# A spectral filter kept and loaded in two halves: forward and backward of a GFNet mixer and a token MLP on one core

## The chip, the core and the metric

The kernel runs on one core of a Trainium2 chip. A core has five engines that run side by side, each with its own instruction queue: TensorE (PE in the profile, its weight loads PEld), VectorE (DVE), ScalarE (ACT), GpSimd (POOL) and SyncE (SP), which here only issues DMAs. ScalarE and GpSimd can issue DMAs too. The DMAs of all of them are carried out by the core's 16 DMA engines. The metric is the device time of one execution in microseconds (us), as the median of several runs.

## The reference, cut to what matters

Forward and backward of two residual blocks over x of 2048 x 448 (bf16). The first block multiplies the two-dimensional real Fourier transform of the normalised input by a complex filter `w_r + 1j * w_i` of 2048 x 225; the second is an MLP over the 2048 tokens.

```python
def _A_ref(x, w_r, w_i):
    X = rfft2(x.astype(float32), axes=(-2, -1))
    W = w_r + 1j * w_i
    X = X * W
    return irfft2(X, s=(S, D), axes=(-2, -1)).astype(bfloat16)

x = A_x
h = x + _A_ref(_layernorm(x), A_w_r, A_w_i)
h2 = h + _B_ref(_layernorm(h), B_w1, B_b1, B_w2, B_b2)   # LN, w1, gelu, w2
_out, _vjp = jax.vjp(_f, A_x, A_w_r, A_w_i, B_w1, B_b1, B_w2, B_b2)
return (out, *vjp(grad_out))
```

The outputs are the result and the gradients of x, w_r, w_i (out_2 and out_3), w1, b1, w2 and b2.

## The kernel before

The transforms are written as matrix products. The forward transform has two parts. In the **row steps** (a loop over t = 0 to 15, lines 932 to 979) PE turns sixteen row tiles of the normalised input with `row_a` and `row_b`; the factor rstd of each tile is scaled into a 128 x 128 matrix by `scale_R` on VectorE, and for tiles 6 to 15 it comes from `newton_gp`, ten small GpSimd instructions for each pair of tiles (lines 410 to 416 in the profile). `fold_prep` and `fold_quarters` on VectorE prepare the operand of two tiles. Every second `row_b` ends with a **row move**, a DMA from SBUF to SBUF into `D2` (line 697), issued by SyncE and, for the last one, by ScalarE. Then comes the **spectral stage** `s2_stage` (line 704): in sets s = 0 to 3 of four groups each, PE transforms down the columns (`four`, 32 x 32 products, line 225), the callback `fwd_mult` multiplies by the filter on VectorE (`w_mult`, two products of 128 x 900 and two sums of 128 x 450, twice a set), PE transforms back, and the results are moved into `D3` by DMAs that GpSimd issues (line 740; in the last set SyncE and ScalarE issue three of the four). Set s uses the groups 8*(s//2) + s%2 + 2a, a = 0 to 3: sets 0 and 1 use groups 0 to 7, sets 2 and 3 groups 8 to 15. After it the inverse row transforms, the MLP, and the same transforms backward follow; there `bwd_mult` also writes the filter's gradient in place over the filter, and it is stored in the last stage.

Between the stages PE is kept going with `fill(n)`, which issues n matmuls of another product, here `dg_gen` (the product of w2 and grad_out, 224 matmuls). Its operand w2 comes in fourteen blocks, five loaded plainly and turned by PE, nine loaded by DMA transposes that SyncE issues (line 312), in a ring of five slots; `cap` holds the later ones back until the row steps are done, and `held_w2` is then emptied.

The instructions of PE, VectorE, ScalarE and SyncE run in the order in which the program writes them. GpSimd's order is chosen by the framework's planner, which simulates the program.

The **filter** lies in `rW`, as component, group and column for each of 128 partitions. `w_io` is a generator that makes one DMA at each `next`; it serves the loads (line 597, from `W_AT` in the row steps) and, at the end, the stores of the gradient (from `GW_AT` in `gx_consumer`). The 64 even partitions hold 16 consecutive rows each, one piece of 7200 bytes; the odd ones hold the mirrored rows, 450 bytes a piece. The move of 16 rows for group 0 of the first odd partitions is the tail. Of the 18 loads 14 are issued by SyncE, and four by GpSimd, each held by a VectorE memset of one element that it overwrites (line 596).

```python
for _ in range(W_AT.get(t, 0)):
    next(w_loads, None)
```

Of the kernel before, what the change touches and what calls it, by code (L numbers as in the profile page):

```python
# [17 lines left out]
P = 128  # L18
S = 2048
D = 448  # L20
DF = 225
# [4 lines left out]
NG = 16  # L26
# [77 lines left out]
class Ring:  # L104
# [7 lines left out]
    def next(self):  # L112
        v = self.views[self.i % len(self.views)]
        self.i += 1
        Ring.release(v)
        return v
# [8 lines left out]
def kernel(  # L125
# [20 lines left out]
    nc = tc.nc  # L146
# [4 lines left out]
    gp_ = nc.gpsimd  # L151
# [9 lines left out]
    def region(name, n):  # L161
        return mem.tile([P, n], BF16, name=name)

    def cut(reg, off, *dims):
        n = int(np.prod(dims))
        v = reg[:, off:off + n]
        if len(dims) == 1:
            return v
        names = "abcd"[:len(dims)]
        return v.rearrange("p (" + " ".join(names) + ") -> p " + " ".join(names),  # L170
                           **{c: d for c, d in zip(names, dims)})
# [59 lines left out]
    def set_of(v, s):  # L231
        return v.rearrange("p (e a c) x k -> p e c a x k", e=2, a=4, c=2)[:, s // 2, s % 2]
# [16 lines left out]
    rW = region("rW", NG * 2 * KW)  # L249
# [157 lines left out]
    def newton_gp(v, y, sl):  # L407
        vi, yi = nt_i[:, 0, sl], y.bitcast(I32)
        a = nt_f[:, 0, sl]
        gp_.tensor_scalar(out=v, in0=v, scalar1=LN_EPS, scalar2=None, op0=ALU.add)  # L410
        gp_.tensor_scalar(out=yi, in0=v.bitcast(I32), scalar1=-0.5, scalar2=RSQRT_MAGIC, op0=ALU.mult, op1=ALU.add)
        for c0, c1 in RSQRT_STEPS:
            gp_.tensor_tensor(out=a, in0=y, in1=y, op=ALU.mult)
            gp_.tensor_tensor(out=a, in0=a, in1=v, op=ALU.mult)
            gp_.tensor_scalar(out=a, in0=a, scalar1=c0, scalar2=c1, op0=ALU.mult, op1=ALU.add)
            gp_.tensor_tensor(out=y, in0=a, in1=y, op=ALU.mult)
# [141 lines left out]
    def gen_inv_d(ch):  # L558
        e, en = inv_cols[ch]
        pt = ps_ff()[:].bitcast(BF16)[:, 0:2 * 2 * P].rearrange("p (w b c) -> p w b c", w=2, b=2)  # L560
        for w in range(2):
            for b in range(2):
                nc.tensor.transpose(pt[0:KC, w, b, :], csF[:, w, b, DC * ch:DC * ch + KC], ident[:])
        for w, x in ((0, e), (1, en)):
            for b in range(2):
                lo = D - DC - DC * b
                for o, i_, f in ((DC * b, pt[0:KC, w, b, 0:DC], e), (lo, pt[0:KC, w, b, DC - 1::-1], x)):
                    o = csI[0:KC, w, ch, o:o + DC]
                    if w:
                        ve.tensor_scalar(out=o, in0=i_, scalar1=f[0:KC], scalar2=None, op0=ALU.mult)  # L570
                    else:
                        sc.activation(out=o, in_=i_, func=ACT.Copy, scale=f[0:KC])

    Wc = cut(rW, 0, 2, NG, DF)
    W = Wc.rearrange("p c g k -> p g c k")

    def w_io(dr, di, store):
        Wq = Wc.rearrange("(q s) c g k -> s q c g k", s=2)  # L580
        for c_, d in ((0, dr), (1, di)):
            moves = []
            for i in range(4):
                moves.append((Wq[0][16 * i:16 * i + 16, c_].rearrange("l g k -> l (g k)"), 16 * i, [[P * DF, 16], [1, 16 * DF]]))
                g0 = 0 if i else 1
                moves.append((Wq[1][16 * i:16 * i + 16, c_, g0:NG, :], P - 16 * i - g0,
                              [[P * DF, 16], [-DF, NG - g0], [1, DF]]))
            moves.append((Wq[1][0:16, c_, 0, :], 64, [[P * DF, 16], [1, DF]]))
            late = [m for n, m in enumerate(moves) if n in (0, 2, 4, 6)] if c_ and not store else []
            early = moves if not late else [m for n, m in enumerate(moves) if n not in (0, 2, 4, 6)]  # L590
            for n, (sb, row, dims) in enumerate(early + late):
                d_ap = bass.AP(d.tensor, d.offset + row * DF, dims)
                eng = nc.sync if n < len(early) else gp_
                if eng is gp_:
                    i = 32 * (n - len(early))
                    nc.vector.memset(Wc[i:i + 1, 1, 8, 0:1], 0.0)
                eng.dma_start(out=d_ap if store else sb, in_=sb if store else d_ap)
                yield

    r452_ring = ring(r452, 0, 8, 2, KW)  # L600
    Xs = cut(rX, 0, NG, 2, KW)
# [151 lines left out]
    def w_mult(xc, w, y, conj):  # L753
        wr = w[:, :, 0:1, :].broadcast_to([P, 2, 2, DF])
        wi = w[:, :, 1:2, :].broadcast_to([P, 2, 2, DF])
        p1, p2 = (p_ring.next()[:, :, :, 0:DF] for _ in range(2))
        xc, y = xc[:, :, :, 0:DF], y[:, :, :, 0:DF]
        ve.tensor_tensor(out=p1, in0=xc, in1=wr, op=ALU.mult)
        ve.tensor_tensor(out=p2, in0=xc, in1=wi, op=ALU.mult)
        ve.tensor_tensor(out=y[:, :, 1, :], in0=p1[:, :, 0, :], in1=p2[:, :, 1, :],  # L760
                         op=(ALU.add if conj else ALU.subtract))
        ve.tensor_tensor(out=y[:, :, 0, :], in0=p1[:, :, 1, :], in1=p2[:, :, 0, :],
                         op=(ALU.subtract if conj else ALU.add))
# [37 lines left out]
    def fill(n):  # L801
        while n > 0 and pending:
            try:
                next(pending[0])
                n -= 1
                if row_ops:
                    row_ops.pop(0)()
            except StopIteration:
                pending.pop(0)
# [12 lines left out]
    def load_biases():  # L822
        gp_.memset(smr, 0.0)
        nc.sync.dma_start(out=gtail[:, 0:64], in_=grad_out[0][S - 16:S, 3 * P:D])
        nc.sync.dma_start(out=smr[0:NFB, 0, :], in_=B_b1.rearrange("(j p) -> j p", p=P))
        nc.sync.dma_start(out=smr[:, 1, :], in_=B_b2.rearrange("(j p) -> j p", p=P))

        def turn():
            for i, dst in ((0, b1col), (1, b2col)):
                nc.sync.dma_start_transpose(out=smc[:, i, :], in_=smr[:, i, :])  # L830

        def place():
            for i, dst in ((0, b1col), (1, b2col)):
                ve.tensor_copy(out=dst[:], in_=smc[:, i, :])
        return turn, place
# [65 lines left out]
    w_loads = w_io(A_w_r, A_w_i, False)  # L901
# [19 lines left out]
    GROUPS = {0: (6, 8), 1: (8, 10), 3: (10, 12), 5: (12, 14), 7: (14, 16)}  # L921
    STATS = {0: (6, 7), 1: (8, 9), **{t: (t + 8,) for t in range(2, 8)}}
    INV_S = {11: 0, 12: 1, 13: 2, 14: 3}
    W_AT = {**{t: 2 for t in range(6)}, 6: 6}
    FILL_A = (4, 4, 8, 12, 6, 3, 3, 4, 5, 3, 3, 2, 2, 2, 3, 3)
    FILL_B = (0, 0, 2, 2, 2, 2, 4, 4, 3, 2, 2, 2, 2, 2, 2, 2)
    def uv_step():
# [4 lines left out]
    for t in range(NT):  # L932
# [34 lines left out]
        if t in GROUPS:  # L967
            a, b = GROUPS[t]
            newton_gp(mvx[:, a:b, 1], rstd_x[:, a:b], slice(a, b))
        for _ in range(W_AT.get(t, 0)):  # L970
            next(w_loads, None)
        if t in INV_S:
            gen_inv_s(INV_S[t])
        if t == 13:
            for c in range(2):
                for e in range(2):
                    sc.copy(out=Rp.rearrange("p (e a q b c) -> p c e a q b", e=2, c=2, q=8, a=2)[:, c, e],
                            in_=Rm[:, 64 * c + 32 * e:64 * c + 32 * e + 32].rearrange("p (q a b) -> p a q b", q=8, a=2))
        fill(FILL_B[t])
    for _ in uv:  # L980
        pass
    for _ in w_loads:
        pass
    gp_.memset(csF[:, 0, :, 0:1], 1.0)
    gen_inv_d(0)
    fill(6)
    gen_inv_d(1)
    turn_biases, place_biases = load_biases()
    cap[0] = NFB
    while held_w2:  # L990
        held_w2.pop(0)()
    fill(4)
    gen_RT()
    fill(7)

    def fwd_mult(s, j, x, y):
        w_mult(x, set_of(W, s)[:, 2 * j:2 * j + 2], y, False)

    s2_stage(lambda s: set_of(Xs, s), fwd_mult, 8, (8,) * 5, 0, split=True)
    sc.activation(out=warm, in_=eps_h, func=ACT.Sqrt)  # L1000
# [99 lines left out]
    for jp in range(NFB // 2):  # L1100
# [27 lines left out]
        d = Later(ve, om_ops) if jp >= NFB // 2 - 2 else ve  # L1128
# [141 lines left out]
    def load_xall(q):  # L1270
        nc.sync.dma_start(out=xall[:, 4 * q:4 * q + 4, :], in_=x_pt[:, 4 * q:4 * q + 4, :])
# [8 lines left out]
    for t in range(NT):  # L1280
# [6 lines left out]
        pb, tmp, m1, m2, _ = ln_a(t, pdh[:, 0:D], rstd_h[:, t:t + 1], hln[:, t, :], (1.0 + LN_EPS) / D)  # L1287
# [10 lines left out]

    def bwd_mult(s, j, xc, y):
        xs = set_of(Xs, s)[:, 2 * j:2 * j + 2, :, 0:DF]  # L1300
        gw = set_of(W, s)[:, 2 * j:2 * j + 2]
        w_mult(xc, gw, y, True)
        xc = xc[:, :, :, 0:DF]
        p1, p2 = (p_ring.next()[:, :, :, 0:DF] for _ in range(2))
        ve.tensor_tensor(out=p1, in0=xc, in1=xs[:, :, 0:1, :].broadcast_to([P, 2, 2, DF]), op=ALU.mult)
        ve.tensor_tensor(out=p2, in0=xc, in1=xs[:, :, 1:2, :].broadcast_to([P, 2, 2, DF]), op=ALU.mult)
        ve.tensor_tensor(out=gw[:, :, 0, :], in0=p1[:, :, 0, :], in1=p2[:, :, 1, :], op=ALU.add)
        ve.tensor_tensor(out=gw[:, :, 1, :], in0=p1[:, :, 1, :], in1=p2[:, :, 0, :], op=ALU.subtract)
# [77 lines left out]
    Meter.slack = 2.0  # L1386
    g_out = w_io(out_2, out_3, True)
    X_AT = {0: 2, 4: 3}
    GW_AT = tuple(range(12)) + tuple(range(1, 12, 2))

    def gx_consumer(t, py):
        if t in X_AT:
            load_xall(X_AT[t])
        for _ in range(GW_AT.count(t)):
            next(g_out, None)
# [87 lines left out]
```

## Time and profile before

| | us |
|---|---|
| median of three runs | 342.39 (342.36 to 346.57) |
| the profiled execution, its own time | 340.34 |
| its span, first to last instruction | 338.3 |

| stretch of the profiled execution | from | to |
|---|---|---|
| filter loads issued by SyncE (14) | 11.5 | 38.5 |
| filter loads issued by GpSimd (4) | 28.6 | 31.1 |
| last row moves issued | 42.2 | 45.4 |
| bias loads issued by SyncE (3) | 45.4 | 47.6 |
| last five w2 transposes issued | 47.7 | 65.0 |
| spectral stage, first to last PE step (line 225) | 48.4 | 69.2 |
| filter gradient stored (18 DMAs) | 289.2 | 321.2 |

A line of the timeline gives the start, the length, the engine and line, the operation, what it writes and reads, how often, and in brackets how long its engine had been idle before it and who ended that. "SPq" and "POOLq" are instructions of a queue that issue or wait. The length of a DMA line is the time that its issue took the queue, not the transfer; the time to landing stands in another view. A line of the stretches gives the bounds and the length, and then for PE, PEld, DVE, ACT and POOL the busy time and the number of instructions, then PE's granted clock, the DMA share and GB/s. Line 84 is a helper through which all of VectorE's and ScalarE's instructions go, line 220 that of the large matmuls, line 225 that of the small ones. Of the tiles, rX holds scaled matrices and later the forward transform, r stands for small regions, rS for work space, rO and rE for w2 blocks.

### The profile page before, as it was taken

The page shows a single profiled execution, that of the slowest core. Times are in us where ns is not written, and L with a number is a line of the kernel's source. Part 1 is how long each engine was busy: PE and PEld are TensorE (multiplying, and loading weights), DVE is VectorE, ACT ScalarE, POOL GpSimd, SP SyncE. Part 2 cuts the span into 40 slices and gives each one's busy share as a digit, 9 for nine tenths or more (in the row PEclk, how much of TensorE's full clock was granted, in tenths as well). Part 3 has the DMA queues.
Part 4 walks back from the last instruction along what each step waited for, and adds up shares of the span by engine and source line. Part 5 has one row for each costly group of instructions (what it writes and reads, how often), then busy time and mean ns, then how long its engine had stood idle before and what let it go on. Part 6 is the DMA issues. An engine that isn't in the chain of part 4 may idle for free.

```text
span 338.3 us, 7987 instructions
## 1 busy us (share of the span) xinstructions
PE 330.2 (98%) x2893; PEld 174.6 (52%) x2893; DVE 251.7 (74%) x670; ACT 206.7 (61%) x448; POOL 84.6 (25%) x254
## 2 busy tenths in 40 slices
PE   8999989999999999999999999999999999999995
PEld 4666554456545555555555555554344434555552
DVE  8998739827947888593227888786697993599994
ACT  6987666848965534423222346665588875588882
POOL 7767202412210000000001111210020222156670
PEclk9999999999999999999999999999999999999999
DMA  7999899959899999687877889837699999978885
GB/s 251 400 203 182 190 258 141 227 125 279 230 378 287 348 279 242 179 274 192 193 178 164 174 188 155 176 84 232 221 220 302 290 244 252 284 188 278 245 293 200
DMA packets 136198, 78.03 MB, mean 231 GB/s; under 512 B 86528, under 2 KB 127592, under 8 KB 136032
## 3 DMA queue, kind: packets, MB, share of 16 engines
q1 hardware_dynamic: 133288, 73.13, 84.5%
q0 software_dynamic: 2448, 3.83, 5.3%
q8 instruction: 22, 0.36, 0.5%
q10 hardware_dynamic: 424, 0.58, 0.5%
q14 instruction: 16, 0.13, 0.1%
HBM read 28.33 MB, written 22.04 MB: 149 GB/s over the span
## 4 chain that ended last, share of the span: by engine, by line
PE 83%; DVE 6%; DMA 4%; ACT 3%; issue 1%; POOL 1%; SPq 0%; DVEq 0%; ACTq 0%
PE ps_mm L220 68%; PE ps_ff L220 9%; PE ps_ff L225 3%; DMA r<-r 3%; ACT rO L84 2%; PE ps_mm L375 2%; DVE rS L84 2%; DVE r L84 1%; DMA r<-rX 1%; DVE rX L84 1%; DVE stats L84 1%; DVE rA L84 1%; ACT rE L84 1%; PE ps_mm L318 0%; DVE rG L84 0%
## 5 line engine op out<-in xcount | busy, mean ns | idle before, releaser
L220 PEld LDWEIGHTS <-r 128*128 128x128 bf16 (+2 forms) x628 | 58.6, 105 | 48.5 <-issue 3.0
L220 PEld LDWEIGHTS <-rS 128*128 128x128 bf16 (+1 forms) x468 | 36.2, 97 | 31.9 <-issue 6.0
L84 ACT CAST rO<-ps_mm 128x512 bf16<-128x512 f32 (+1 forms) x68 | 36.5, 584 | 14.5 <-PE ps_mm L220 11.9
L220 PE MATMUL ps_mm<-rD,r 128*128 128x448 bf16 x224 | 44.5, 352 | 0.0
L220 PEld LDWEIGHTS <-rst 128*128 128x128 bf16 (+1 forms) x320 | 23.9, 97 | 30.4 <-issue 12.1
L740 POOL DMA_DIRECT2D r<-r x29 | 17.4, 605 | 67.3 <-ACT r L84 56.7
L220 PE MATMUL ps_mm<-rC,rE 128*128 128x448 bf16 x144 | 32.1, 353 | 0.0
L220 PE MATMUL ps_mm<-rB,r 128*128 128x448 bf16 x160 | 31.2, 352 | 0.2 <-DVE rB L84 0.2
L220 PE MATMUL ps_mm<-rG,rst 128*128 128x512 bf16 (+1 forms) x128 | 28.5, 380 | 0.0
L220 PE MATMUL ps_mm<-r,rst 128*128 128x512 bf16 (+2 forms) x144 | 27.3, 345 | 0.0
L84 ACT ACTIVATE r<-ps_mm,rstd_h 128x448 bf16<-128x448 f32 x16 | 10.1, 634 | 26.8 <-PE ps_mm L220 26.8
L84 DVE SCALAR_TENSOR_TENSOR r<-ps_mm,b2col,r 128x448 bf16<-128x448 f32 x16 | 10.9, 682 | 19.9 <-PE ps_mm L220 18.6
L84 ACT ACTIVATE r<-rC 128x448 bf16<-128x448 bf16 x16 | 9.1, 570 | 26.7 <-DMA out_dram<-r 13.8
L84 ACT CAST r<-ps_ff 128x452 bf16<-128x452 f32 x43 | 23.1, 592 | 3.1 <-PE ps_ff L220 1.2
L1220 POOL TENSOR_SCALAR lcol<-lcol 128x1 f32<-128x1 f32 x16 | 8.5, 530 | 64.7 <-ACT r L84 64.7
L84 ACT ACTIVATE rG<-rG 128x896 bf16<-128x896 bf16 x14 | 13.3, 950 | 14.9 <-DVE rG L84 14.7
L220 PEld LDWEIGHTS <-rO 128*128 128x128 bf16 (+1 forms) x165 | 15.4, 98 | 12.3 <-ACT rO L84 0.2
L84 ACT CAST rS<-ps_ff 128x512 bf16<-128x512 f32 x31 | 18.0, 583 | 4.2 <-PE ps_ff L220 4.2
L220 PE MATMUL ps_ff<-csI,rAT 113*128 113x224 bf16 (+1 forms) x108 | 19.0, 298 | 0.2 <-DVE rA L84 0.2
L84 ACT CAST rG<-ps_mm 128x512 bf16<-128x512 f32 (+1 forms) x28 | 14.0, 539 | 7.6 <-PE ps_mm L220 7.5
L84 ACT CAST rAT<-ps_ff 113x512 bf16<-113x512 f32 x24 | 13.9, 586 | 7.7 <-PE ps_ff L220 7.5
L84 DVE TENSOR_SCALAR rG<-rG 128x896 bf16<-128x896 bf16 x28 | 10.9, 389 | 10.0 <-ACT rG L84 10.0
(200 smaller groups left out, 647.4 us busy)
## 6 DMA issues: line engine op xcount, KB each, us to landing
out_dram<-rO SPq DMA_DIRECT2D x34, 256.0 KB, 3.3
r<-in_B_w_dram SPq DMA_DIRECT2D x5, 1024.0 KB, 9.1
r<-r POOLq DMA_DIRECT2D x29, 113.0 KB, 5.5
out_dram<-rG SPq DMA_DIRECT2D x11, 256.0 KB, 3.1
r<-in_B_w_dram SPq DMA_DIRECT2D x3, 896.0 KB, 5.6
rS<-in_B_w_dram SPq DMA_DIRECT2D x3, 896.0 KB
rB<-in_B_w_dram SPq DMA_DIRECT2D x5, 512.0 KB, 8.1
r<-r SPq DMA_DIRECT2D x11, 226.0 KB, 2.5
```

The costliest lines, as they stand in the source:

```text
L84: fn(**kw)
L220: nc.tensor.matmul(out, lhsT=lhsT, rhs=rhs, start=start, stop=stop)
L225: nc.tensor.matmul(out, lhsT=lhsT, rhs=rhs, start=start, stop=stop)
L375: nc.tensor.matmul(idle[:, 0:D], lhsT=rAT[:, 0:P], rhs=rAT[:, 0:D], start=True, stop=True)
L740: defer(RESH_LAG, lambda g=g, ab=ab, eng=eng: eng.dma_start(out=D3[rowbase(g):rowbase(g) + 29:4, :, :, :], in_=ab), ab)
L1220: gp_.tensor_scalar(out=m1, in0=ms, scalar1=-1.0 / D, scalar2=None, op0=ALU.mult)
```

## The change

The filter is kept as two halves of eight groups, each with both components: half 0 serves sets 0 and 1, half 1 sets 2 and 3. `w_set(s)` gives the view that `set_of(W, s)` gave. `w_io` goes through half 0 and then half 1; in each it moves, for each component, all 64 even-partition rows in one DMA (pieces of 3600 bytes; the DRAM side has the dimensions 4, 16 and the piece), then four DMAs of the odd partitions, and in half 0 the tail. That is 22 DMAs instead of 18. In the row steps `W_AT` now takes the twelve of half 0, all from SyncE, in steps 0 to 8. The ten of half 1 stand behind the row steps, after the table scaling `gen_inv_d` and after the held w2 loads; two are issued by SyncE and eight by GpSimd, and all are held by one VectorE memset of two elements in each partition. The bias loads move behind them. The stores are taken from `GW_AT` as before, but 22 of them, all from SyncE.

```diff
-    Wc = cut(rW, 0, 2, NG, DF)
-    W = Wc.rearrange("p c g k -> p g c k")
+    Wc = rW[:, 0:2 * NG * DF].rearrange("p (e c g k) -> p e c g k", e=2, c=2, g=NG // 2)
+
+    def w_set(s):
+        return Wc[:, s // 2].rearrange("p c (a b) k -> p b a c k", b=2)[:, s % 2]
 
     def w_io(dr, di, store):
-        Wq = Wc.rearrange("(q s) c g k -> s q c g k", s=2)
-        for c_, d in ((0, dr), (1, di)):
-            moves = []
-            for i in range(4):
-                moves.append((Wq[0][16 * i:16 * i + 16, c_].rearrange("l g k -> l (g k)"), 16 * i, [[P * DF, 16], [1, 16 * DF]]))
-                g0 = 0 if i else 1
-                moves.append((Wq[1][16 * i:16 * i + 16, c_, g0:NG, :], P - 16 * i - g0,
-                              [[P * DF, 16], [-DF, NG - g0], [1, DF]]))
-            moves.append((Wq[1][0:16, c_, 0, :], 64, [[P * DF, 16], [1, DF]]))
-            late = [m for n, m in enumerate(moves) if n in (0, 2, 4, 6)] if c_ and not store else []
-            early = moves if not late else [m for n, m in enumerate(moves) if n not in (0, 2, 4, 6)]
-            for n, (sb, row, dims) in enumerate(early + late):
-                d_ap = bass.AP(d.tensor, d.offset + row * DF, dims)
-                eng = nc.sync if n < len(early) else gp_
-                if eng is gp_:
-                    i = 32 * (n - len(early))
-                    nc.vector.memset(Wc[i:i + 1, 1, 8, 0:1], 0.0)
-                eng.dma_start(out=d_ap if store else sb, in_=sb if store else d_ap)
-                yield
+        Wq = Wc.rearrange("(q s) e c g k -> s q e c g k", s=2)
+        H = NG // 2
+        for e in range(2):
+            for c_, d in ((0, dr), (1, di)):
+                up, dn = Wq[0][:, e, c_], Wq[1][:, e, c_]
+                moves = [(up.rearrange("q g k -> q (g k)"), H * e, [[16 * DF, 4], [P * DF, 16], [1, H * DF]])]
+                for i in range(4):
+                    g0 = 0 if e or i else 1
+                    moves.append((dn[16 * i:16 * i + 16, g0:H], P - 16 * i - H * e - g0,
+                                  [[P * DF, 16], [-DF, H - g0], [1, DF]]))
+                if not e:
+                    moves.append((dn[0:16, 0], 64, [[P * DF, 16], [1, DF]]))
+                for n, (sb, row, dims) in enumerate(moves):
+                    eng = gp_ if e and n and not store else nc.sync
+                    d_ap = bass.AP(d.tensor, d.offset + row * DF, dims)
+                    eng.dma_start(out=d_ap if store else sb, in_=sb if store else d_ap)
+                    yield
...
-    W_AT = {**{t: 2 for t in range(6)}, 6: 6}
+    W_AT = {0: 2, 1: 1, 2: 2, 3: 1, 4: 2, **{t: 1 for t in range(5, 9)}}
...
-    for _ in w_loads:
-        pass
     gp_.memset(csF[:, 0, :, 0:1], 1.0)
     gen_inv_d(0)
     fill(6)
     gen_inv_d(1)
-    turn_biases, place_biases = load_biases()
     cap[0] = NFB
     while held_w2:
         held_w2.pop(0)()
+    nc.vector.memset(Wc[:, 1, :, 0, 0:1], 0.0)
+    for _ in w_loads:
+        pass
+    turn_biases, place_biases = load_biases()
...
-    GW_AT = tuple(range(12)) + tuple(range(1, 12, 2))
+    GW_AT = tuple(range(12)) + tuple(range(1, 11))
```

More of the change, by code (lines that the diff above doesn't have):

```diff
@@ L996, in fwd_mult @@
     def fwd_mult(s, j, x, y):
-        w_mult(x, set_of(W, s)[:, 2 * j:2 * j + 2], y, False)
+        w_mult(x, w_set(s)[:, 2 * j:2 * j + 2], y, False)
     s2_stage(lambda s: set_of(Xs, s), fwd_mult, 8, (8,) * 5, 0, split=True)
@@ L1300, in bwd_mult @@
         xs = set_of(Xs, s)[:, 2 * j:2 * j + 2, :, 0:DF]
-        gw = set_of(W, s)[:, 2 * j:2 * j + 2]
+        gw = w_set(s)[:, 2 * j:2 * j + 2]
         w_mult(xc, gw, y, True)
```

## The prediction

> **What bounds the kernel now.** First the page's engine table, then the chain that ended last, then the timelines of GpSimd, VectorE and SyncE's queue around the filter loads, then stretches of PE.
>
> ```profile
> PE 330.2 (98%) x2893; PEld 174.6 (52%) x2893; DVE 251.7 (74%) x670; ACT 206.7 (61%) x448; POOL 84.6 (25%) x254
> ```
>
> PE is all but full and its order is fixed, so a change that leaves PE's work alone gains only where PE stands or drags. The stretches say where: PE idles 0.68 us in 32-36, 0.06 in 36-40, 0.52 in 44-48 and 0.39 in 48.0-48.4: 1.65 us between the row steps and the first step of the spectral stage.
>
> ```profile
> 32.00:36.00 4.00, 3.32 (x37) 1.89 (x38) 2.57 (x10) 2.99 (x6) 2.65 (x14) 1.00 1.00 203
> 44.00:48.00 4.00, 3.48 (x22) 1.78 (x20) 1.92 (x10) 2.50 (x10) 0.04 (x1) 1.00 0.95 334
> ```
>
> The chain (start, length, what) names the cause: from 34.0 to 36.2 it runs through GpSimd's rstd steps, then a VectorE fold, and at the end through the last row move.
>
> ```profile
> 33.59 0.41 PE ps_ff L220 x4
> ...
> 35.97 0.21 POOL rstd_x L416
> ...
> 36.20 0.89 DVE rX L84 x2
> ...
> 43.01 1.23 DVE rX L84 x2
> 44.24 0.47 SPq L697
> ...
> 44.81 3.45 DMA r<-rX
> ...
> 48.40 0.72 PE ps_ff L225 x24
> ```
>
> GpSimd's timeline has the four filter loads inside that rstd work; VectorE waits behind it twice; SyncE's queue is busy without a break from 37.3 to 65.
>
> ```profile
> 28.57 1.76 POOL L597 DMA_DIRECT2D rW<-in_A_w_i_dram  x3
> 30.54 0.53 POOL L597 DMA_DIRECT2D rW<-in_A_w_i_dram  x1
> 33.38 0.25 DVE L84 TENSOR_SCALAR rX<-Rm,rstd_x 128x128 bf16<-128x128 bf16 x1 [0.81 <-POOL rstd_x L416]
> 36.20 0.32 DVE L84 TENSOR_SCALAR rX<-Rm,rstd_x 128x128 bf16<-128x128 bf16 x1 [0.78 <-POOL rstd_x L416]
> 39.29 2.78 SPq L312 DMA_TRANSPOSE rO<-in_B_w_dram  x1
> 42.17 1.23 SPq L697 DMA_DIRECT2D r<-r  x2
> 59.47 1.17 DVE L84 TENSOR_TENSOR rS<-rX,rW 128x900 bf16<-128x900 bf16 x2
> ```
>
> **Row steps.** Removed: four GpSimd loads (1.76 + 0.53 = 2.3 us) and four one-element VectorE fills (0.41 us at 27.97). The rstd group of tiles 12-13 had begun at 26.66 and lacked three steps at 28.57; without the loads it ends near 29.5 instead of 33.35, so the first VectorE wait (0.81) goes. The PE stall at 35.02 (0.66 us, ended by the fold behind that wait) goes with it: 0.7 us. The group of tiles 14-15 needs statistics that come at 31.3, takes ten steps of some 0.28 us, and could end near 34.2 instead of 36.17. That frees the second wait (0.78), and the fold before PE at 38.44, where weights waited 0.50 us: I take 0.5. Against it: GpSimd's order is the planner's, and a memset of csF that waits for PE (34.05, after 0.56 idle) sits in this group. If it still cuts in before the last seven steps, the 0.5 is 0. So 1.2 us, bounds 0 and 2.1 (PE's 1.65 idle plus 0.5 hidden in pipelined records).
>
> **SyncE's queue in the row steps.** 14 loads become 12, nine ahead of the third w2 transpose instead of twelve (3 x 0.62 = 1.9 us of issue less), and one, the last, falls between the fourth transpose (39.29) and the five back-to-back row moves that begin at 42.17. If that queue still sets the last move, this costs 0.65 us (one issue); if the transposes start sooner, as fewer loads ahead of them suggest, nothing. I take nothing: the last move follows its casts, which come 1.2 us earlier, and PE's wait for its landing (0.91 at 48.40) stays.
>
> **The second half.** Its ten loads wait for a VectorE memset (60 ns) that stands after the table scaling ending at 47.95; with the gain, 46.8. GpSimd issues eight loads of 128 pieces. The nearest row is its own moves of 128 pieces, L740: 0.60 us to issue, 5.8 to 6.9 us to land beside the transposes. The eighth is issued at 46.8 + 7 x 0.6 = 51.0 and lands by 57.9. Nothing else is on GpSimd until 56.87. SyncE now issues two w2 transposes first (45.45 + 1.9 + 3.7, with gaps 51.2; 1.2 earlier with the row moves, 50.0), then the two 64-row loads (0.62 each), then the three bias loads (2.2 us, moved here; used only after 80). VectorE first needs the half at 59.47 and its imaginary part 0.6 later: 58.3 and 58.9 with the gain.
>
> Plain loads behind a transpose landed 4.1 to 6.6 us after issue. The shape adds to this: two SyncE moves of eight outer rows (71-74.8 us) made 272 packets, that is 2 x 128 and 2 x 8 closing ones, where a move over 32 partitions closes with 16. The 64-row load has an outer count of four on the DRAM side, by the same pattern four engines with 16 packets of 3600 bytes each. The packet records show 140 ns for one of 3584 bytes: 2.2 us a load, 4.5 the pair, where sixteen engines would take 1.1: 3.4 more for the second. So that one, issued at 50.6, lands between 58.1 and 60.6, in the middle at 59.4: a wait X of 0.5 us, bounds 0 and 1.7. Set 2's product would end at 63.46 + X, set 3's would start then instead of 64.01, and PE takes set 3's result right as it comes (68.51), so all but 0.55 of X is lost: I charge 0.2, bounds 0 and 1.2. [...]
>
> **Behind it.** The last three w2 transposes move behind two more issues (1.24 us) and start 1.2 earlier. The last landed at 70.3, PE uses it at 71.88, 1.2 earlier with the gain: slack 0.3. I charge 0.2, bounds 0 and 3.3: with the pair's 4.5 us of data ahead it comes 4.2 too late, of which PE's idle 0.9 at 75.3 (it waits there for the moves into D3) swallows as much. Products and gradients read the new layout in the same shapes (0.63 us each): nothing. Stores grow from 18 to 22, four more issues of 0.62 us on SyncE between 289 and 321, where it waits for others again and again (5.1 us for one line alone): nothing, at most 2.5 if that cover were gone.
>
> **Sum.** -1.2 + 0.2 + 0.2 = -0.8 us on the profiled execution (span 338.3, 340.34 with what lies around it): 339.5. The runs' median is 342.39, 2.05 above that execution, so 341.6.
>
> **Rivals.** (1) *No gain* (0.20): the planner keeps the memset in the rstd steps, or the row moves stay behind SyncE's queue with the tail load ahead of them. For it: five moves back to back. Against: three fewer loads ahead. The 0.7 stall spent on the 0.65 issue gives 342.3, the cost alone 343.0. (2) *The second half is late* (0.23, of it 0.03 beyond 2%), the case on the other side: VectorE waits at set 2 for the 64-row loads. If the second transpose takes the 5.26 us of the last one, the second load is issued at 52.1 and lands 6.6 + 3.4 later at 62.1: X = 3.2, 2.65 lost, with the rest of the sum 343.9. If the queue gains nothing as well, 63.3: 345.1. It decides from a landing near 60.7, where the gain is used up. For it: four engines, and DMA at 9 tenths in most slices there. Against: the transposes leave gaps in which the loads can run. (3) *Late w2* (0.08): PE waits 3.3 for the last transpose: 342.4 + 3.3 - 1.2 = 344.5. (4) *More gain* (0.10): the last move lands sooner too, as no GpSimd packets and fewer loads stand before the row moves; 2.1 go: 340.3, with 0.4 of VectorE's removed fills on top 339.9.
>
> **Numbers.** Forecast 341.6 (0.39), its own range 340.8 to 342.2. The 8-in-10 range runs from 339.9 (case 4) to 345.1 (cases 2 and 3). Two per cent, about what a measurement of this kernel can tell, is 6.8 us: no gain term reaches it (0.01, for what I do not see); slower needs X above 8.4 (0.04).
>
> **What would show it.** Right: no GpSimd load before 44, both VectorE waits for rstd gone, first L225 step near 47.2, the first product of set 2 waiting under 1 us. Wrong: first L225 at 48.4 or later with SyncE's moves still back to back (case 1); VectorE idle before set 2 for longer, released by a DMA into rW (case 2); PE idle near 70 for rO (case 3).

## The result, and the profile after

| | before | after |
|---|---|---|
| median, runs on the same chip | 341.53 (6 runs) | 354.79 (6 runs) |
| the profiled execution, its own time | 340.34 | 357.65 |
| its span | 338.3 | 355.8 |

The changed kernel is slower: the ratio is 1.041 (95% interval 1.036 to 1.046), 13.3 us by the medians. The two profiled executions lie 17.3 us apart, 4 more than the medians, since the one of before was a quick one of its kind and the one of after the longest of its six; what follows places the 17.3 and sizes the causes by medians where it can.

First the page of after: PE's busy time is 2.7 us more than before although its work is the same, and the row of the granted clock has a hole in the slices from 53 to 71 us (in the page of before it is 9 throughout).

```profile
PE 332.9 (94%) x2893; PEld 175.3 (49%) x2893; DVE 250.9 (71%) x667; ACT 206.4 (58%) x448; POOL 84.0 (24%) x258
...
PEclk9999996599999999999999999999999999999996
```

The row steps did what was forecast. In the stretches PE is busy through 32-36, where it stood 0.68 us before:

```profile
32.00:36.00 4.00, 4.00 (x68) 2.82 (x66) 2.92 (x11) 3.54 (x8) 2.29 (x11) 1.00 0.84 195
```

VectorE's timeline holds the loss. One wait for GpSimd in the row steps is left, 1.05 us, now for a memset of csF behind the last rstd step; the other is gone. Then, after the cast at 48.78, VectorE does nothing until 60.65, and what it then begins is the filter product of **set 0**, which needs the first half only. The first line is that product in the profile of before, where it waits for nothing; the others are of after:

```profile
51.41 1.17 DVE L84 TENSOR_TENSOR rS<-rX,rW 128x900 bf16<-128x900 bf16 x2
```

```profile
34.71 0.32 DVE L84 TENSOR_SCALAR rX<-Rm,rstd_x 128x128 bf16<-128x128 bf16 x1 [1.05 <-POOL csF L982]
...
46.41 0.06 DVE L989 MEMSET rW<- 128x2 bf16 x1
48.78 0.62 DVE L84 CAST rD<-ps_mm 128x448 bf16<-128x448 f32 x1 [2.11 <-PE ps_mm L220]
60.65 1.17 DVE L84 TENSOR_TENSOR rS<-rX,rW 128x900 bf16<-128x900 bf16 x2 [11.25 <-DMA rW<-in_A_w_i_dram]
```

The chain of waits goes the same way, from the memset over GpSimd's loads to the last of them, issued at 50.7 and landed at 60.2:

```profile
46.79 0.78 POOL rW L597
47.57 3.15 POOL rW L597 x6
50.72 9.52 DMA rW<-in_A_w_i_dram
...
60.65 1.18 DVE rS L84 x2
```

PE runs out of fill at 52.8, stands until 62.6, and then eight matmuls of 128x448 take 3.17 us where eight of the same shape took 1.69 before the pause: the clock is at one half from 56.0 to 69.7.

```profile
51.08 1.69 PE L220 MATMUL ps_mm<-rC,rO 128*128 128x448 bf16 x8
62.61 0.57 PE L225 MATMUL ps_ff<-rS,UVT 32*32 32x452 bf16 x8 [9.85 <-DVE rS L84]
...
65.56 3.17 PE L220 MATMUL ps_mm<-rC,rO 128*128 128x448 bf16 x8
```

The second loss is in the last stage. SyncE's queue has issues of the filter's stores that take 3.44 and 2.81 us for two, and the store of the x gradient behind them (L1432) goes out late. The first line shows two such stores in the profile of before, the others are of after:

```profile
319.93 1.31 SPq L597 DMA_DIRECT2D out_dram<-rW  x2
```

```profile
323.44 3.44 SPq L597 DMA_DIRECT2D out_dram<-rW  x2
...
334.72 2.81 SPq L597 DMA_DIRECT2D out_dram<-rW  x2
337.62 1.27 SPq L1267 DMA_TRANSPOSE rst<-rB  x1
338.99 0.52 SPq L1432 DMA_DIRECT2D out_dram<-r  x1
```

VectorE stands 2.97 us before a step that writes `r`, the buffers that the x gradient's stores read, and PE then waits 3.91 us for VectorE. The line of after names a ScalarE step as the releaser. The same step of the run "no pad", told below, stands 2.61 us with the store named, and in before it doesn't wait. The three lines are of before, after and no pad, and then comes PE in after:

```profile
324.35 0.44 DVE L84 SCALAR_TENSOR_TENSOR r<-ps_ff,rstd_x,r 128x224 bf16<-128x224 f32 x1
```

```profile
341.40 0.45 DVE L84 SCALAR_TENSOR_TENSOR r<-ps_ff,rstd_x,r 128x224 bf16<-128x224 f32 x1 [2.97 <-ACT rO L84]
```

```profile
336.16 0.45 DVE L84 SCALAR_TENSOR_TENSOR r<-ps_ff,rstd_x,r 128x224 bf16<-128x224 f32 x1 [2.61 <-DMA out_dram<-r]
```

```profile
348.83 2.95 PE L220 MATMUL ps_mm<-r,rst 128*128 128x512 bf16 x13 [3.91 <-DVE rG L84]
```

To place losses in all runs alike I matched PE's matmuls in order with those of the profile of before and took the difference of their starts at four of them, named by their time before: 50.4 (first filter products under way), 88.4 (spectral stage over), 298.4 (last stage, few stores issued yet) and 333.6 (end). Positive is later. (The last four traces, no half 2 to 12 stores, lack nine matmul records, which the match leaves out.) The runs were made in four sessions, each with its own runs of before, and each ratio goes by these. A row reads: gain of the row steps; plus loss in the spectral stage; plus what comes until 298; plus the end.

| run | median, ratio to before (95%) | at 50.4 | at 88.4 | at 298.4 | at 333.6 |
|---|---|---|---|---|---|
| after | 354.79, 1.041 (1.036 to 1.046) | -2.04 | +10.74 | +11.55 | +16.35 |
| two tiles | 353.39, 1.038 (1.028 to 1.047) | -1.45 | +5.38 | +5.50 | +10.86 |
| all early | 353.31, 1.037 (1.028 to 1.046) | +7.76 | +8.67 | +9.73 | +13.54 |
| loads SyncE | 343.93, 1.012 (1.004 to 1.020) | +3.18 | +2.55 | +3.19 | +3.19 |
| tiles, 16 rows | 349.68, 1.029 (1.020 to 1.038) | -1.93 | +5.89 | +6.65 | +8.59 |
| no pad | 351.93 (one run) | -1.69 | +8.11 | +8.71 | +10.94 |
| old stores | 346.11, 1.015 (1.009 to 1.020) | -0.46 | +6.66 | +7.09 | +7.09 |
| 4 GpSimd late | 344.15, 1.008 (1.004 to 1.012) | +6.85 | +6.54 | +6.54 | +6.54 |
| 8 GpSimd late | 341.82, 0.999 (0.996 to 1.003) | +1.25 | +0.82 | +1.54 | +1.54 |
| no half 2 | 339.63, 0.999 (0.994 to 1.003) | -1.68 | -1.96 | +1.30 | +1.30 |
| all GpSimd | 344.41, 1.010 (1.005 to 1.016) | -1.73 | +2.46 | +2.77 | +2.77 |
| no pad only | 341.54, 1.001 (0.997 to 1.005) | -0.53 | +0.33 | +0.24 | +0.24 |
| 12 stores | 343.82, 1.008 (1.004 to 1.011) | -0.82 | -1.09 | -1.21 | +1.24 |

For after: 2.04 us gained, 11.25 of waiting and some 2 us of half clock lost, 0.6 won back, 0.8 lost near 290, 4.8 lost at the end, and the last 1 us of the 17.3 from there on, where the clock was at one half again from 349.6.

### The profile page after: what moved, and what is told of

It reads as the page before. It is cut to its first block, busy times and chain, and to the rows that moved or that the text cites. A ratio compares the mean times of both kernels' runs of the same rounds, so it can differ in the third digit from the quotient of the medians.

```text
span 355.8 us, 7998 instructions
## 1 busy us (share of the span) xinstructions
PE 332.9 (94%) x2893; PEld 175.3 (49%) x2893; DVE 250.9 (71%) x667; ACT 206.4 (58%) x448; POOL 84.0 (24%) x258
## 4 chain that ended last, share of the span: by engine, by line
PE 79%; DMA 7%; DVE 5%; ACT 3%; issue 2%; POOL 1%; SPq 1%; ACTq 0%; DVEq 0%
PE ps_mm L220 67%; PE ps_ff L220 8%; PE ps_ff L225 3%; DMA rW<-in_A_w_i_dram 3%; DMA rB<-in_B_w_dram 2%; ACT rO L84 2%; DVE r L84 2%; DMA r<-r 2%; POOL rW L597 1%; DVE rS L84 1%; SPq L329 1%; PE ps_ff L318 1%; DVE rA L84 1%; ACT csI L84 1%; DVE rG L84 1%
## 5 line engine op out<-in xcount | busy, mean ns | idle before, releaser
L220 PEld LDWEIGHTS <-r 128*128 128x128 bf16 (+2 forms) x628 | 58.6, 104 | 48.8 <-issue 4.0
L220 PE MATMUL ps_mm<-r,rst 128*128 128x512 bf16 (+2 forms) x144 | 28.6, 356 | 4.2 <-DVE rG L84 3.9
L220 PEld LDWEIGHTS <-rO 128*128 128x128 bf16 (+1 forms) x165 | 15.7, 100 | 13.3 <-issue 1.7
L84 ACT ACTIVATE rG<-rG 128x896 bf16<-128x896 bf16 x14 | 13.3, 950 | 14.9 <-DVE rG L84 14.7
L84 DVE TENSOR_TENSOR rS<-rX,rW 128x900 bf16<-128x900 bf16 x16 | 9.4, 630 | 14.5 <-DMA rW<-in_A_w_i_dram 11.3
L220 PE MATMUL ps_mm<-rC,rO 128*128 128x448 bf16 x80 | 19.4, 375 | 0.0
```

What stands on the lines that cost most here:

```text
L84: fn(**kw)
L220: nc.tensor.matmul(out, lhsT=lhsT, rhs=rhs, start=start, stop=stop)
```

## The experiments

**Two tiles.** Why does set 0 wait for a half that it doesn't read? In the compiled program the first product of set 0 waits on the semaphores of all eight GpSimd loads and both SyncE loads of the second half; even the memset at 46.41, two elements a partition of the second half, waits on the semaphore of a load of the first, which it doesn't in the two runs that follow. The first theory was that one tile is tracked as one thing.

```diff
-    rW = region("rW", NG * 2 * KW)
+    rW0, rW1 = region("rW0", NG * KW), region("rW1", NG * KW)
```

> The changed kernel with the two halves in two tiles of their own; the loads, their queues and their order are the same. Tracking theory (the first product of set 0 was held for the second half's landings only because both halves lie in one tile): the 11.3 us wait ahead of the first product goes, PE stays at clock 1.0 through 56-70, VectorE waits at set 2's product instead, for about 2 to 3 us (last landings near 60.2, needed near 57.4), and of the 12.8 us that the spectral stage lost some 10 to 12 come back: 343 to 345.5 us if the 4.6 us at the end stay lost. Data theory (the loads of the second half themselves slow what set 0 needs, its own landings or its operands): the wait stays within 2 us of 11.3 and the time near 354.5.

The wait ahead of set 0 went. The profiled execution is 5.5 us shorter than that of after, but the median only 1.4 us, far less than expected and no more than the intervals of the two ratios allow for nothing (1.036 to 1.046 and 1.028 to 1.047). The wait had a second one beneath it, at the first product of set 2, and VectorE's timeline has it at 6.04 us:

```profile
57.15 0.70 DVE L84 TENSOR_TENSOR rS<-rS 128x450 bf16<-128x450 bf16 x2
63.90 1.17 DVE L84 TENSOR_TENSOR rS<-rX,rW 128x900 bf16<-128x900 bf16 x2 [6.04 <-DMA r<-r]
```

The releaser that is named, a move, is not it: GpSimd's moves there landed from 65.58 on, but the last GpSimd load of the second half landed at 63.58, 0.3 us before the product began. It was issued at 51.31: 12.3 us for 56 KB.

**No pad.** The finer cause of the tracking. The tile is 7,232 elements long and 7,200 are used.

```diff
-    rW = region("rW", NG * 2 * KW)
+    rW = region("rW", NG * 2 * DF)
```

> The changed kernel with one edit: the filter's tile is 7,200 elements long, as long as what is used of it, where it was 7,232; the 32 unused ones at the end go. Theory (the two halves are one tile whose rows are longer than the view, so an access to all partitions of one half counts as touching the other half too, and the program makes set 0 wait for it): the first product waits for the first half alone, the 11 us wait moves to set 2 and is 5 to 7 us there, as with two tiles; 351 to 354. Rival (a tile is always tracked as a whole): the first product still waits for the second half, 354 to 356.

Both halves in one tile, and set 0 no longer waits; the wait is at set 2's imaginary product.

```profile
49.66 1.16 DVE L84 TENSOR_TENSOR rS<-rX,rW 128x900 bf16<-128x900 bf16 x2
...
61.68 0.63 DVE L84 TENSOR_TENSOR rS<-rX,rW 128x900 bf16<-128x900 bf16 x1 [3.35 <-DMA rW<-in_A_w_i_dram]
```

This is one run, so its time isn't compared; the waits are what it shows. A tile isn't tracked as a whole. An access through a view shorter than the tile's rows, over all partitions, was taken to touch the rest; 32 unused elements made the false dependency. PE then lost 4.44 and 1.24 us waiting for blocks of w2, rival 3 of the prediction.

**Tiles, 16 rows.** Why do the loads land so late? The DMA view of after from 50 to 61 us (its first row: busy share of the 16 engines in 40 slices of 0.275 us, in tenths; below, an issue line with its median time to landing):

```profile
DMA  0100999695997999922323922321222223399999
...
rW<-in_A_w_i_dram POOLq DMA_DIRECT2D x3, 56.2 KB, 9.8
```

From 54.7 to 59.6 the engines are at 1 to 3 tenths but for one slice, about four of sixteen, while loads of GpSimd and a transpose are outstanding. The 128 packets of 3600 bytes of SyncE's two 64-row loads run from 51.5 to 59.2, exactly four at a time for 5.2 of these 7.7 us. Of the 128 packets of GpSimd's loads 108 had ended by 54.7; the other 20 ran beside them up to 58.0. The first load of the pair ends with four packets of 4 bytes, at 55.46 to 55.65. Both agree with the prediction's estimate of four engines for an outer count of four. The edit puts four loads with an outer count of 16 in the place of each:

```diff
+                if e and not store:
+                    moves = [(up[16 * i:16 * i + 16].rearrange("q g k -> q (g k)"), H + 16 * i, [[P * DF, 16], [1, H * DF]]) for i in range(4)]
```

> The kernel of the two tiles with each 64-row load of the second half cut into four loads of 16 rows on SyncE (the stores stay). If the four engines that a 64-row load runs on are what holds the loads queued behind it: landings of the second half end some 3 to 5 us earlier, the wait at set 2 falls below 1 us, and 1 to 2.5 us come off the two-tile kernel: 341.5 to 343.5. If the transposes or the number of packets set the landings: the same landings within 1 us, and the six further issues on SyncE (3.7 us) push the bias loads and w2's last transposes back: equal or up to 2 us slower than the two tiles.

```profile
DMA  0000799399969594999993738455835969995799
...
rW<-in_A_w_i_dram POOLq DMA_DIRECT2D x3, 56.2 KB, 5.9
```

The trough is gone, the same GpSimd loads take 5.9 us in place of 9.8, the last of them landed at 56.73, and VectorE waits 0.75 at set 2. The median fell by 3.7 and the profiled time by 2.9; the intervals of the two ratios overlap (1.020 to 1.038 and 1.028 to 1.047). But PE now stands for w2, whose third transpose is issued at 56.57, behind six more loads and the bias loads:

```profile
67.03 0.56 PE L220 MATMUL ps_mm<-rC,rE 128*128 128x448 bf16 x1 [4.52 <-DMA rE<-in_B_w_dram]
```

**All GpSimd** (built on old stores, below). Are the transposes late because of their place in SyncE's queue, or because of the data?

```diff
-                    eng = gp_ if e and n >= nup else nc.sync
+                    eng = gp_ if e else nc.sync
```

> The run with the old stores, but all sixteen loads of the second half from GpSimd, none from SyncE, so w2's transposes follow one another at once on SyncE. If SyncE's eight issues ahead of the transposes cost the w2 wait: that wait goes, the second half's last loads are issued 4 us later and VectorE waits 1 to 3 us at set 2: 341.5 to 343.5. If the DMA engines have no room for both in this stretch: transposes slow down again (5 us and more each on the queue), one wait takes the place of the other, 344.5 to 347.

The wait for w2 went, and VectorE waits 4.31 us at set 2 instead, longer than expected:

```profile
62.60 0.63 DVE L84 TENSOR_TENSOR rS<-rX,rW 128x900 bf16<-128x900 bf16 x1 [4.31 <-DMA rW<-in_A_w_i_dram]
```

One transpose took 5.03 us on SyncE's queue again. 344.41 stands between the two expectations. The queue's order moved the wait from w2 to the filter, and room is short either way. Whether the order won time is open: the median is 1.7 us less than with SyncE's loads, but 0.7 of that lies between the two medians of before, and the intervals overlap (1.005 to 1.016 and 1.009 to 1.020).

**No half 2** (on old stores). The ceiling: what could the move bring if the second half cost nothing?

```diff
-                for n, (sb, row, dims) in enumerate(moves):
+                for n, (sb, row, dims) in enumerate(() if e else moves):
```

> The run with the old stores (346.1), its ten-load second half left out: that half of the filter is never read from memory, GpSimd fills it with zeros while it is idle near 37 to 44, so the outputs of half the groups lack their filter. Theory (data of the second half beside w2's transposes is what delays both): the waits of VectorE at set 2 and of PE for w2 near 67 go, the row steps' gain of 0.7 to 1.5 us is all that is left: 339.5 to 341. Rival (w2's transposes are late because they are issued behind the moved lines, not because of the data): PE still waits 2 us or more for w2, 342 to 344.

(The half left out has sixteen loads in this form; GpSimd fills its place with zeros, so the outputs lack that half of the filter.) Both waits are gone, the row steps' 1.7 us are kept through 281 us, and the median is 339.63 against 340.70 in the same session, 0.9986 with an interval that reaches from 0.994 to 1.003. So the most that the change could have brought is about 1 us by the medians and 2 by the interval; loading the second half's 0.9 MB, in a stretch where the DMA row of before is mostly at 9 tenths, cost the rest. In the profiled execution 3.3 us were lost again near 287: PE waited 1.96 us for moves into another buffer, before any store of the filter, and the clock was at one half from 288.8 to 292.2. Why there is not shown.

**Old stores.** The second half as in tiles, 16 rows, but layout and 18 stores of before (their places in the diff), in one tile without the pad.

```diff
-    GW_AT = tuple(range(12)) + tuple(range(1, 11))
+    GW_AT = tuple(range(12)) + tuple(range(1, 12, 2))
```

> The kernel with 16-row loads of the second half (349.7), but in the layout and with the 18 stores at the places of the kernel before; one tile without the 32 unused elements. Store theory (the 22 stores in halves are what backs SyncE up in the last stage): the loss at the end, 2.7 us there, and the 0.8 near 290 to 300 go, 346 to 347.5. Rival (the late w2 weights and shifted queues cause the end's loss): 349 to 350. The wait of PE for w2's transposes near 67 (4.5 us) stays in both.

The median fell by another 3.6, and the table places 1.9 of them: nothing is lost behind 298.4 (7.09 and 7.09), where the run with 22 stores loses 1.9. The rest is not placed, since the profiled execution of this run was the longest of its four (347.69).

**12 stores.** Count or shape? The kernel before with fewer stores, two of 64 rows.

```diff
+            if store:
+                moves = [(Wq[0][:, c_].rearrange("q g k -> q (g k)"), 0, [[16 * DF, 4], [P * DF, 16], [1, 16 * DF]])] + moves[1:8:2] + moves[8:]
...
-    GW_AT = tuple(range(12)) + tuple(range(1, 12, 2))
+    GW_AT = tuple(range(12))
```

> The kernel before with 12 stores of the filter's gradient in place of 18: the four 16-row stores of each part become one of 64 rows (an outer count of four on the memory side), one store a step. If the shape is what backs SyncE up at the end (a store on four engines, 64 packets of 7200 bytes on 4 of 16): stores and moves behind it land late, 343.5 to 346. If the count of issues does it: six issues fewer, 340.5 to 341.8.

Six issues fewer and yet 2.4 us lost behind 298.4; the median is 3.1 above before. Stores of other outputs behind them are held: the x gradient's stores (L1433 here; L1431 before, where the one landing on record took 3.4) land after up to 9.7 us, and VectorE waits for one:

```profile
DMA to landing us min/median/max: 1.9/5.8/9.7
```

```profile
317.75 0.45 DVE L84 SCALAR_TENSOR_TENSOR r<-ps_ff,rstd_x,r 128x224 bf16<-128x224 f32 x1 [3.41 <-DMA out_dram<-r]
```

Across the table, the five runs with 64-row stores that were profiled (after, two tiles, all early, tiles 16 rows, no pad) and this one lose 1.9 to 5.4 us behind 298.4; the seven with 16-row stores lose none. So the shape is enough to do it. In after the packets of the first 64-row store run four at a time for 2.06 of its 2.22 us, those of the other three for 2.82 to 2.85 of 3.7 to 4.4 us. The changed kernel with nothing but its stores cut to 16 rows was not run.

**All early.** The changed kernel with everything loaded by SyncE in the row steps.

```diff
-                    eng = gp_ if e and n and not store else nc.sync
+                    eng = nc.sync
...
-    W_AT = {0: 2, 1: 1, 2: 2, 3: 1, 4: 2, **{t: 1 for t in range(5, 9)}}
+    W_AT = {t: 2 for t in range(11)}
```

> The changed kernel with all 22 loads issued by SyncE in the row steps, two a tile step, so nothing of the filter is loaded in the spectral stage; layout, stores and products as in the changed kernel. Store theory (22 stores on SyncE, two of them of 64 rows, delay the stores of the last stage): the last stage still loses 2 to 4.6 us against the kernel before, the row steps keep 1 to 2 us of gain: 342 to 344.5. Consequence theory (the loss at the end came from the stall and the halved clock early on): no loss at the end, 339.5 to 340.5.

The end loses 3.8 us, as the store theory has it. The front was a miss of the expectation: 22 loads and the transposes in one queue push the last row moves to 46.9-51.5 (40.5-42.8 in after), and PE waits for their landing, 7.69 us before its first spectral step. This wait isn't the filter's.

**Loads SyncE, 4 GpSimd late, 8 GpSimd late.** Three versions of the kernel before without GpSimd loads among the rstd steps: the four issued by SyncE; the four behind the last rstd step; eight there, with ten left to SyncE.

```diff
-                eng = nc.sync if n < len(early) else gp_
+                nc.sync.dma_start(out=d_ap if store else sb, in_=sb if store else d_ap)
```

> The kernel before, its four GpSimd loads and their fills replaced by issues from SyncE at the same places; one set of 18 loads and 18 stores, old layout. If the row steps' gain comes from freeing GpSimd and VectorE there: both VectorE waits for rstd and PE's stall at 35 go, 1 to 2 us less: 339.5 to 340.5. If it came from SyncE's shorter queue (fewer loads ahead of the transposes and moves): no gain, 341.5 to 342.5, with the first product step of the spectral stage at 48.4 or later.

```diff
+        for c_, i in ([(c, i) for c in (1,) for i in range(0, P, 32)] if tail else []):
+            gp_.tensor_copy(out=Wc[i:i + 1, c_, 8, 0:1], in_=rstd_x[i:i + 1, 15:16])
+        for c_, d, (sb, row, dims) in tail:
+            gp_.dma_start(out=sb, in_=bass.AP(d.tensor, d.offset + row * DF, dims))
```

> The kernel before with its four GpSimd loads put behind GpSimd's last rstd step (near 36) instead of among them, the four fills moved to GpSimd there, and the tile without the unused elements; SyncE's 14 loads stay. If GpSimd's loads in the rstd steps cost the row steps 1 to 2 us and nothing else hangs on them: 339.5 to 340.8. Rival (their packets now run beside the row moves at 37 to 48 and delay the last one): PE waits longer at the first spectral step, 341.5 to 343.

```diff
-        for c_, i in ([(c, i) for c in (1,) for i in range(0, P, 32)] if tail else []):
+        for c_, i in ([(c, i) for c in (0, 1,) for i in range(0, P, 32)] if tail else []):
```

> As the run before, but eight loads behind GpSimd's last rstd step (the four of the real part too), so SyncE has ten in the row steps instead of 14. If SyncE's queue ahead of the row moves also holds the spectral stage's start (four issues fewer, 2.5 us): 338.5 to 340, with the first spectral step of PE near 46. Rival (the eight loads' data, 0.46 MB, beside the row moves): the last move lands no earlier, or the first product waits for a filter load: 340.5 to 343.

None is faster than before. With the four on SyncE the row steps themselves win 1.3 us (1.40 late at 17.6, 0.06 late at 46.2), and then PE stands 2.92 us before its first spectral step. With the four late on GpSimd it stands 6.57 us, since the last row move, issued at 48.8, landed at 53.75:

```profile
53.89 0.81 PE L225 MATMUL ps_ff<-r,Vt 32*32 32x452 bf16 x12 [6.57 <-DMA rst<-in_B_b_dram]
```

(The line names a bias load as the releaser; by the times it is the move, which that step of PE reads.) With eight late and four fewer on SyncE, SyncE's moves are issued by 42.7, 2.1 us sooner than before, but one issued at 38.4 landed only at 45.1, PE still waits 2.27, and the time is that of before. What is won by taking the loads out of the rstd steps is lost again to row moves that land late.

**No pad only**, a control for the runs that include it.

```diff
-    rW = region("rW", NG * 2 * KW)
+    rW = region("rW", NG * 2 * DF)
```

> The kernel before with one edit, the 32 unused elements of the filter's tile taken away. The first product waits there for loads that landed before 44, so the finer tracking should be worth nothing: 341 to 342 (as before within 0.5%). If it is worth something by itself (say 1 us or more either way), the runs that include it have to be read against this one.

The ratio is 1.001 (0.997 to 1.005): by itself it is worth nothing.

## Why the prediction was wrong

**Row steps: right.** Forecast were 1.2 us; 1.49 were won by 46.2 and 2.04 by 50.4, and 1.45 to 1.93 in five of the six other runs that kept these loads (0.46 in old stores, which was 0.65 late at 17.6 already). One of the two waits stayed (1.05 us), by the memset that the prediction had named against itself.

**SyncE in the row steps: better than "nothing".** The last moves went out 2.6 us earlier, and PE's wait of 0.91 us for them, which was to stay, went; that is the 0.8 above the forecast.

**Second half: the step that failed.** "VectorE first needs the half at 59.47" is true of the data and false of the program. The prediction took the order of accesses for the order of waits. The first product, next in VectorE's queue at 49.4, waited 11.25 us for the landing at 60.2. With what a product waits for read from the program, the forecast's own landings (58.1 to 60.6) would have given most of the loss, though partly by luck: that range was for SyncE's second 64-row load, and the load that landed at 60.2 was the last of GpSimd's. Two more errors lay under it. X at set 2, 0 to 1.7 with 3.2 as the worst, was 6.0 (two tiles) and 3.35 us (no pad) once set 0 was free. The 64-row pair wasn't the cause in the way that was charged: its last packet ended at 59.0 to 59.6 in these runs and after, inside the range. GpSimd's loads, on another queue, were put down to land by 57.9. They landed at 60.2 (after), 63.6 (two tiles) and 61.5 (no pad), and at 56.7 in tiles, 16 rows, where the pair is gone. Their last packets ended at 58.0, 57.1 and 56.6, and at 54.7 there: beside the pair the data came 2 to 3 us later. From the last packet to the landing it is 2 us in after and in tiles, 16 rows, but 6.5 in two tiles and 4.9 in no pad; what took this time is not shown. And the clock was no term of the sum: half speed cost some 2 us after the pause.

**Late w2: mis-sized.** Charged 0.2, at most 3.3. In after it is hidden under the larger stall; in tiles, 16 rows, where the half comes in time, it is 4.5.

**Stores: failed.** They were counted ("four more issues of 0.62 us") and their shape was not looked at, though the same text had worked out four engines for the loads. The end lost 4.8 us in the profile of after against "at most 2.5", and 3.6 us of median went with the old stores.

**Rivals.** The one on the other side, the second half late, had the right resource and the wrong place and price: set 2 and 343.9 to 345.1 (344.0 to 345.2 when its terms are added again) against set 0 and 354.8. By medians, undone on top of each other: 1.4 us for the false dependency alone, 3.7 for the four engines of the loads, 3.6 for the old layout and stores, 1.7 for SyncE's order, and 4.8 for having this half's data there at all. The 1.4, the 3.7 and the 1.7 lie within the overlap of their intervals; for these parts the waits in the traces are the evidence, not the times. Another order of undoing would share them out otherwise. What makes the profiled execution of after 3 us longer than its median stays open (its mean granted clock, 0.972, is the lowest of the six, 0.975 to 0.984 in the others), as do the 0.1 to 0.8 us that most runs lose between 281 and 298.

## What to carry to other kernels

Before a part of a buffer is loaded later, read in the compiled program what its first reader waits on: a view shorter than its tile can tie the two parts together. Look at the outer count of every DMA: the 64-row loads, with a count of four, ran four packets at a time for 5.2 of 7.7 us, GpSimd's loads beside them took 9.8 us to land in place of 5.9, and behind 64-row stores those of the x gradient took up to 9.7 (12 stores). And in a stretch where the DMA engines are full, leave the transfer out once: that run costs little and shows what moving it can bring at most.

## What had not been expected of the hardware

The half clock came in whole steps. The spells of granted clock 0.5 that follow a pause of PE lasted 3.41 us (six runs, two tiles among them), 6.83 (tiles, 16 rows, no pad and 4 GpSimd late), 10.24 (all early) and 13.65 (after): one, two, three and four times 3.41. In after the clock fell 3.3 us after PE's last matmul ended and rose 7.1 us after it had begun again. The stretches show how little PE did until then (3.37 us of four between 64 and 68, and 0.57 in the four before):

```profile
60.00:64.00 4.00, 0.57 (x8) 0.12 (x7) 3.17 (x7) 0.00 (x0) 0.00 (x0) 0.50 1.09 240
64.00:68.00 4.00, 3.37 (x47) 1.52 (x48) 3.72 (x9) 1.85 (x4) 1.68 (x3) 0.50 0.50 113
```

By the ends that the trace models, PE worked 0.14 us in the 3.41 us before that fall, and 0, 0.24, 1.97 and 3.41 us in the four stretches of 3.41 us from there to the rise. A pause of 1.07 us at 299.4 in the same profile was followed by no half clock; 1.96 us in no half 2 and 2.27 in 8 GpSimd late were each followed by 3.41 us of it. The loss in no half 2 was 3.3 us, more than the pause itself, and in after 7 us of slow matmuls followed the one of 9.85. How long a pause has to be is not shown.

The other surprise is reach. Two 64-row loads of SyncE, four packets at a time for 5.2 of 7.7 us, stretched GpSimd's loads, from a queue of its own, from 5.9 to 9.8 us, and a DMA transpose behind them stood 7.3 us on SyncE's queue in after and 8.3 in two tiles, where most took 2 to 5. The pair isn't the whole reason for the transposes: in no pad two that were issued after the pair's last packet stood 8.2 and 7.6 us, and why is not shown.
